# Attention into a maxout layer on one core: other buffers, one group of filler products less and earlier loads of q and k in the first batch

## Chip, core and metric

The kernel runs on one NeuronCore of a Trainium2 chip. The metric is the device time of one execution in microseconds (us), lower is better; the median of the runs counts.

## The reference

Attention with a causal window of 128 positions and a linear position penalty per head, for 8 batches, 8 heads, 576 positions and head size 64, and behind it a maxout layer:

```python
scores = q @ k.T / sqrt(64) - slope[h] * |i - j|      # only 0 <= i - j < 128
attn = softmax(scores)
x = concat_heads(attn @ v)                            # 4608 tokens x 512
h = max(x @ w1, x @ w2, x @ w3)                       # 768 wide
out = h @ w_out                                       # 512 wide
```

All data are float32. The linear layers are done in three products of split operands each (high x low, low x high, high x high).

## The kernel before

A **task** is a pair of heads of one batch (32 tasks, four to a batch, `NP = 4`). A **step** is one block of 128 query rows of a task; the steps of two tasks make 9, so a batch has 18 (`n_steps`). For a step, TensorE makes the score products (`products`, L431; on steps 2, 6, 10 and 14 of a batch whole 128x256 blocks to `ps_m`, else to `ps_s`), VectorE merges the two key blocks by a mask (`score`, L447 and L450) and takes bias and row minimum into a tile `s` (L461), ScalarE makes the exponentials into a tile `p` with their sums (`exps`, L473). For each two steps the sums are inverted (L479, L480) and `p` is scaled, one of the two by GpSimd (L487), the other by ScalarE (L492). Four steps later TensorE transposes `p` (`turn`, L500, into the single PSUM tile `pt`), ScalarE copies it out as `pr` or `pp` (L504, L509, L512), GpSimd cuts it to the window with two selections for a step (L520, L524), and TensorE multiplies with `v` (`mix`, L545, into `ps_x`; L567 in later batches). ScalarE copies the result out as `xk` (L552).

`plain_x` (through `split`, L614 on ScalarE and L615 on VectorE) splits `xk` in a high and a low part `xs`, the right operand of the linear layer. In batches 0 and 1 the layer is done plainly: `plain`, L791, in units of 12 products of 128x288, four units for each of nine groups of weights and eight more for the output layer. The first halves of three units are done early (`begin_early`, L767). From batch 2 on, seven products replace eight (`unit`, L846), with combined weights.

The weights come as 12 groups in int64 words (`fetch`, L152, tile `hs`, two buffers `hs2`) and are turned into floats in pieces between the rest (`preparing`): a clamp (L166 on VectorE, for the later groups L170 and L171 on ScalarE), a conversion (L177, L181), three pieces of bit work (L186), a cast (L200, ScalarE) and a difference (L203, VectorE) into `ring` or `ow`; the floats and the split ones are stored to DRAM (L327, L216).

`spin` (L375) adds products of zeros to `pt`, in fours, whose results nobody reads: at the start, at steps 3, 5, 7 and so on of batch 0, and ten before the second unit of `plain`.

The order of the work is a list of events with due times in steps (`at`, at the end of the function). In batch 0 a scheduler moves instructions from there: it fills each engine's queue by what it believes to be ready, so that buffers and loads change the order. From the due time 46 on (in batch 2) the order on TensorE is that of the list.

q and k of a task lie in one tile `qk` (`load`, L394, two buffers), v in `v` (`load_v`, L399, two buffers). All these loads, the weights' loads and the stores are issued by one queue, SyncE's, in order: a transfer whose buffer is not yet free holds up those behind it. A task's q and k are asked for at step 1 of the task two before, its v at step 3 of the task before. Pools: `s_p` holds `s` (3 buffers), `p` (4) and `pr` (2); `xs_p` has 7 buffers for the factors `xs`; `hq_p` 7 for the hidden units `hq` (128x288); `t_p` 10 for `t` (128x288).

Of the kernel before, what the change touches and what calls it, by code (L numbers as in the profile page):

```python
# [8 lines left out]
F32 = mybir.dt.float32  # L9
# [10 lines left out]
LOAD_I = 1  # L20
# [17 lines left out]
def attention_maxout_kernel(  # L38
# [12 lines left out]
    P = 128  # L51
    B, NP, _, _, S = qk.shape
# [5 lines left out]
    NB = S // P  # L58
# [3 lines left out]
    qk_p = ctx.enter_context(tc.tile_pool(name="qk_p", bufs=2))  # L62
    v_p = ctx.enter_context(tc.tile_pool(name="v_p", bufs=2))
    s_p = ctx.enter_context(tc.tile_pool(name="s_p", bufs=3))
    pp_p = ctx.enter_context(tc.tile_pool(name="pp_p", bufs=4))
    xk_p = ctx.enter_context(tc.tile_pool(name="xk_p", bufs=1))
    xs_p = ctx.enter_context(tc.tile_pool(name="xs_p", bufs=7))
    hq_p = ctx.enter_context(tc.tile_pool(name="hq_p", bufs=7))
    hs_p = ctx.enter_context(tc.tile_pool(name="hs_p", bufs=7))
    t_p = ctx.enter_context(tc.tile_pool(name="t_p", bufs=10))  # L70
# [76 lines left out]
    def raw_tile():  # L147
        return hs_p.tile([P, SMALL + 4 * DM], I32, name="hs2", bufs=2)

    def fetch(g):  # L150
        r = raws[g] = raw_tile()
        nc.sync.dma_start(r[:, SMALL:].bitcast(U8)[:, :16 * DM - 3], w_all[g].bitcast(U8)[:, 3:])  # L152
# [233 lines left out]
    tasks = [(b, hp) for b in range(B) for hp in range(NP)]  # L386
    qkt, vt = {}, {}


    def load(t):  # L390
        b, hp = tasks[t]
        qkt[t] = qk_p.tile([P, 2, S], F32, name="qk")
        for cs in (slice(0, 2 * P), slice(2 * P, S)) if t == 0 else (slice(0, S),):
            nc.sync.dma_start(qkt[t][:, :, cs], qk[b, hp, :, :, cs])  # L394

    def load_v(t):
        b, hp = tasks[t]
        vt[t] = v_p.tile([P, NB + 1, P], F32, name="v")
        nc.sync.dma_start(vt[t], v[b, hp])  # L399

    pn, pp, xp, xk, stats = {}, {}, {}, {}, {}
# [8 lines left out]
    n_steps = len(steps) // B  # L410
# [27 lines left out]
    def score(s):  # L438
        t, i = steps[s]
        b, hp = tasks[t]  # L440
        ps, a = banks.pop(s)
        first = tc.keep_in_program_order if s < 4 else lambda x: x
        if i:
            mask = prev[:, i == NB].bitcast(mybir.dt.uint8)
            if a is None:
                for x in ps:
                    first(nc.vector.copy_predicated(x[:, P:2 * P], mask, x[:, :P]))  # L447
            else:
                both = scores[:, :, a * 2 * P:(a + 1) * 2 * P]
                first(nc.vector.copy_predicated(  # L450
                    both[:, :, P:], mask.unsqueeze(1).broadcast_to([P, 2, P]), both[:, :, :P],
                ))

        if s % 2 == 0:
            stats[s // 2] = st_p.tile([P, 3, 2, 2], F32, name="st")
        st = stats[s // 2]
        less[s] = []
        for j in range(2):
            x = s_p.tile([P, P], F32, name="s", bufs=3)
            below = bias_t[:, hp // 2, j] if i == NB else (bias if i else bias0)[:, 2 * hp + j, :]  # L460
            first(nc.vector.tensor_tensor_reduce(  # L461
                out=x, in0=ps[j][:, P:2 * P], in1=below,
                scale=-0.125, scalar=3.0e38, op0=ALU.add, op1=ALU.min, accum_out=st[:, 0, s % 2, j:j + 1],
            ))
            less[s].append(x)
# [2 lines left out]

    def exps(s):
        st, a = stats[s // 2], s % 2  # L470
        p = pn[s] = s_p.tile([P, 2, P], F32, name="p", bufs=4)
        for j, x in enumerate(less.pop(s)):
            nc.scalar.activation(  # L473
                p[:, j], x, AF.Exp, bias=st[:, 0, a, j:j + 1], scale=-1.0, accum_out=st[:, 1, a, j:j + 1]
            )
# [134 lines left out]
    xs, hs, hq = {}, {}, {}  # L610
# [261 lines left out]
    def at(when, what, *args):  # L872
        events.append((when, len(events), what, args))
# [2 lines left out]
    where = {x: s for s, x in enumerate(steps)}  # L876
    for s, (t, i) in enumerate(steps):
        c = s + shift[tasks[t][0]]
        if i == LOAD_I and t + 2 < len(tasks):
            at(c - 0.4, load, t + 2)  # L880
        if i == NB - 1 and t + 1 < len(tasks):
            at(c - 0.4, load_v, t + 1)
        if i == 0 and 0 < t < NP:
            at(c - 1, slopes, t)
            if t % 2 == 0:
                at(c - 1, slopes_t, t // 2)
        at(c + 0.04, score, s)
        at(c + 0.3, exps, s)
        if s % 2 == 0:
            at(c + 0.002, products, s)  # L890
            at(c + DRAIN[0].get(n_steps - s, LAG_T) + 0.003, turn, s)
        else:
            at(c + (0.6 if s == n_steps - 1 else 1.1), sums_of, s)
            at(c + (0.8 if s == n_steps - 1 else 1.5), normalise, s)
# [34 lines left out]
    at(2.06, weights, 1)  # L929
    for s in range(5, n_steps + 2):  # L930
        at(s + 0.2, weights, 1.4 if s > 5 else 0.6)
    for s in range(3, n_steps, 2):
        at(s + 0.45, spin, SPIN)

    def fix():
# [3 lines left out]
    at(2 * n_steps + LAG_X + shift[2], fix)  # L939
    spin(FIRST_SPIN)  # L940
    load(0)
    nc.scalar.dma_start(dist[:, 2], c_ident)
    fetch(0)
    slopes(0)
    slopes_t(0)
    load(1)
    load_v(0)
    nc.scalar.copy(out=plus, in_=dist[:, 2])
    fetch(1)
    for _, _, what, args in sorted(events, key=lambda e: e[:2]):  # L950
        what(*args)

# [37 lines left out]
```

## Time and profile before

| | |
|---|---|
| median of 3 runs | 750.1 us (749.47 to 752.38) |
| the profiled execution | 752.57 us, span from first to last instruction 750.9 us |
| mean granted TensorE clock | 0.995 of full speed |
| TensorE products, busy | 733.9 us (98%) |
| TensorE weight loads, busy | 674.6 us (90%) |
| VectorE, ScalarE, GpSimd, busy | 515.2, 487.2 and 236.4 us |
| DMA | 192.81 MB, mean 257 GB/s |

The span has three parts: the attention of batch 0 until about 57 us, the plain layer of batches 0 and 1 mixed with the attention of later batches, and the layer with combined weights. PE is TensorE's products, PEld its weight loads, DVE VectorE, ACT ScalarE, POOL GpSimd, SPq the queue of SyncE. TensorE's busy time is modelled from starts, since products overlap. float32 products of `L431`, `L500` and `L545` appear as two records each in the trace.

### The profile page before, as it was taken

How to read it: one execution, taken by the hardware profiler on the slowest of the kernel's cores; microseconds unless marked ns; L12 is line 12 of the kernel's file. 1: busy time of each engine (PE TensorE's matmuls, PEld its weight loads, DVE VectorE, ACT ScalarE, POOL GpSimd, SP SyncE). 2: the span in 40 equal slices, each digit the busy share in tenths (PEclk: the TensorE clock that was granted, in tenths of full speed). 3: DMA queues.
4: the chain of work that ended last, by engine and by line, in shares of the span. 5: the costliest groups of instructions: out<-in, count | busy, mean ns of one | idle time of the engine just before them, and what ended most of it. 6: DMA issues, size and time to landing. Idle time of an engine off the chain costs nothing.

```text
span 750.9 us, 19281 instructions
## 1 busy us (share of the span) xinstructions
PE 733.9 (98%) x7209; PEld 674.6 (90%) x7214; DVE 515.2 (69%) x1614; ACT 487.2 (65%) x1603; POOL 236.4 (31%) x451
## 2 busy tenths in 40 slices
PE   7999989999999999999999999999999999999998
PEld 3459988999999999999999999999999999999998
DVE  4888887536659477784778567794777747683673
ACT  5786976766667767676677757776666767552342
POOL 4661224645556123212222123222222122343100
PEclk8999999999999999999999999999999999999999
DMA  7877999759998489855988378864988468899611
GB/s 252 274 282 298 330 340 331 253 187 340 361 349 275 134 279 303 273 181 192 322 294 276 116 266 304 291 213 146 330 289 273 163 228 272 252 291 355 230 61 64
DMA packets 57085, 192.81 MB, mean 257 GB/s; under 512 B 5792, under 2 KB 24480, under 8 KB 50464
## 3 DMA queue, kind: packets, MB, share of 16 engines
q0 software_dynamic: 20304, 108.54, 43.9%
q1 hardware_dynamic: 36400, 82.85, 31.2%
q8 instruction: 57, 0.93, 0.5%
q14 instruction: 36, 0.29, 0.1%
q10 hardware_dynamic: 288, 0.20, 0.1%
HBM read 156.95 MB, written 34.60 MB: 255 GB/s over the span
## 4 chain that ended last, share of the span: by engine, by line
PE 77%; DVE 11%; ACT 7%; DMA 2%; issue 1%; POOL 1%; SPq 0%; DVEq 0%; ACTq 0%; POOLq 0%
PE ps_m L846 46%; PE ps_m L791 16%; PE ps_s L431 5%; PE pt L500 4%; PE ps_x L567 4%; DVE hs L615 2%; DVE hq L733 2%; ACT p L473 2%; DVE t L732 2%; DMA qk<-in_qk 1%; PE ps_x L545 1%; DMA hs<-in_w_all 1%; ACT p L492 1%; DVE t L618 1%; DVE xs L615 1%
## 5 line engine op out<-in xcount | busy, mean ns | idle before, releaser
L846 PE MATMUL ps_m<-xs,ring 128*128 128x288 f32 x2160 | 302.7, 297 | 0.6
L846 PEld LDWEIGHTS ps_m<-xs,ring 128*128 128x128 f32 x2160 | 290.1, 188 | 3.7 <-ACT t L863 3.4
L520 POOL TENSOR_SCALAR_AFFINE_SELECT pp<-pr 128x256 f32<-128x256 f32 x112 | 53.9, 482 | 277.2 <-ACT pr L504 154.0
L473 ACT ACTIVATE p<-s,st 128x128 f32<-128x128 f32 x288 | 114.7, 400 | 20.8 <-DVE st L461 17.2
L863 ACT COPY t<-ps_m 128x288 f32<-128x288 f32 x196 | 76.7, 394 | 71.2 <-PE ps_m L846 69.5
L791 PE MATMUL ps_m<-xs,ring 128*128 128x288 f32 x846 | 118.1, 297 | 2.8 <-DVE hq L808 2.2
L791 PEld LDWEIGHTS ps_m<-xs,ring 128*128 128x128 f32 x846 | 113.3, 188 | 4.1 <-DVE hq L808 2.4
L367 POOL DMA_DIRECT2D ring<-keep x103 | 55.5, 539 | 165.5 <-PE ps_m L846 157.3
L846 PE MATMUL ps_m<-hs,ow 128*128 128x288 f32 x756 | 105.8, 297 | 0.4
L846 PEld LDWEIGHTS ps_m<-hs,ow 128*128 128x128 f32 x756 | 100.9, 188 | 2.6 <-ACT t L863 1.2
L492 ACT ACTIVATE p<-p,st 128x128 f32<-128x128 f32 x252 | 84.6, 393 | 24.1 <-DVE st L480 24.1
L732 DVE TENSOR_TENSOR t<-ps_m,t 128x288 f32<-128x288 f32 x108 | 48.8, 453 | 42.8 <-PE ps_m L846 32.5
L461 DVE CUSTOM_DVE_ANT_0 s<-ps_s,bias 128x128 f32<-128x128 f32 x240 | 60.6, 285 | 9.0 <-POOL bias_t L112 3.4
L431 PE MATMUL ps_s<-qk 64*64 64x192 f32 (+1 forms) x1088 | 62.0, 319 | 3.4 <-DMA qk<-in_qk 2.4
L614 ACT CAST hs<-hq 128x288 fp32r<-128x288 f32 x96 | 40.2, 432 | 30.8 <-DVE hq L733 18.1
L473 ACT ACTIVATION_READ_ACCUMULATOR p<-s,st 128x1 f32 x288 | 55.3, 192 | 0.0
L567 PE MATMUL ps_x<-pp,v 64*64 64x64 f32 (+3 forms) x1456 | 53.4, 274 | 0.1
L567 PEld LDWEIGHTS ps_x<-pp,v 64*64 64x64 f32 x1456 | 41.7, 133 | 10.5 <-issue 8.6
L500 PE MATMUL pt<-plus,p 128*128 128x128 f32 x288 | 48.5, 289 | 2.0 <-POOL p L487 1.3
L524 POOL TENSOR_SCALAR_AFFINE_SELECT pp<-pr 128x256 f32<-128x256 f32 (+1 forms) x112 | 50.0, 447 | 1.1
L733 DVE TENSOR_TENSOR hq<-t,hq 128x288 f32<-128x288 f32 x108 | 48.8, 457 | 2.1
L601 DVE TENSOR_TENSOR xk<-ps_x,xk 128x256 f32<-128x256 f32 (+3 forms) x56 | 25.4, 454 | 36.0 <-ACT xk L600 36.0
(94 smaller groups left out, 942.0 us busy)
## 6 DMA issues: line engine op xcount, KB each, us to landing
ring<-keep POOLq DMA_DIRECT2D x51, 1024.0 KB, 7.4
ring<-keep POOLq DMA_DIRECT2D x61, 768.0 KB, 6.1
qk<-in_qk SPq DMA_DIRECT2D x31, 576.0 KB, 5.3
hs<-in_w_all SPq DMA_DIRECT2D x12, 1023.6 KB, 7.2
v<-in_v SPq DMA_DIRECT2D x32, 320.0 KB, 6.5
outT<-t SPq DMA_DIRECT2D x64, 144.0 KB, 1.8
keep<-ring SPq DMA_DIRECT2D x9, 768.0 KB, 6.5
plain<-hs SPq DMA_DIRECT2D x12, 512.0 KB, 4.0
```

The lines of the kernel that those rows point to most:

```text
L367: nc.gpsimd.dma_start(wts[n, a], keep[n % 9][a])
L431: pe(nc.tensor.matmul(ps[j][d:d + D, o:o + k1 - k0], lhsT=qkt[u][j * D:(j + 1) * D, 0, q0:q0 + D], rhs=qkt[u][j * D:(j + 1) * D, 1, k0:k1] ...
L461: first(nc.vector.tensor_tensor_reduce(out=x, in0=ps[j][:, P:2 * P], in1=below, scale=-0.125, scalar=3.0e38, op0=ALU.add, op1=ALU.min, acc ...
L473: nc.scalar.activation(p[:, j], x, AF.Exp, bias=st[:, 0, a, j:j + 1], scale=-1.0, accum_out=st[:, 1, a, j:j + 1])
L492: nc.scalar.activation(p[:, j], p[:, j], AF.Copy, scale=st[:, 2, a, j:j + 1])
L500: pe(nc.tensor.transpose(out=pt[:, a, j], in_=p[:, j], identity=ident))
L567: pe(nc.tensor.matmul(x[j * D:(j + 1) * D, r, o:o + rhs.shape[1]], lhsT=vv[k, i, j * D:(j + 1) * D], rhs=rhs[k], start=start, stop=True, s ...
L732: nc.vector.tensor_tensor(out=s, in0=ps, in1=e, op=ALU.add)
L733: nc.vector.tensor_tensor(out=h, in0=s, in1=h, op=ALU.max)
L791: pe(nc.tensor.matmul(ps, lhsT=lt, rhs=rt, start=n == 0 and not (b == 0 and v < EARLY), stop=n == len(pairs) - 1, skip_group_check=True,))
L846: pe(nc.tensor.matmul(part_of[n, {2: 0, 5: 0, 6: 0, 3: 1}.get(kk, kk)], lhsT=lt, rhs=rt, start=first, stop=i == len(pairs) - 1, skip_group ...
L863: nc.scalar.copy(out=e, in_=ps)
```

## The change

In batch 0 the tile `s` is taken from `hq_p` (7 buffers) and `p` from `t_p` (10 buffers), which nothing else uses there yet. The filler products of step 5 go. q and k of tasks 2 and 3 are loaded at the beginning, to two of the factors' seven buffers, and with them v of task 1; the loads of the steps keep tasks 4 and up. In the changed file the lines from `load` on are one higher, from `exps` on two higher (L394 is L395, L431 is L432, L473 is L475, L487 is L489, L500 is L502, L545 is L547, L615 is L617, L767 is L769, L791 is L793).

```diff
     def load(t):
         b, hp = tasks[t]
-        qkt[t] = qk_p.tile([P, 2, S], F32, name="qk")
+        own = 2 <= t < NP
+        qkt[t] = (xs_p if own else qk_p).tile([P, 2, S], F32, name="xs" if own else "qk")
...
         for j in range(2):
-            x = s_p.tile([P, P], F32, name="s", bufs=3)
+            x = s_p.tile([P, P], F32, name="s", bufs=3) if b else hq_p.tile([P, P], F32, name="hq")
...
         st, a = stats[s // 2], s % 2
-        p = pn[s] = s_p.tile([P, 2, P], F32, name="p", bufs=4)
+        first = s < n_steps
+        p = pn[s] = t_p.tile([P, 2, P], F32, name="t") if first else s_p.tile([P, 2, P], F32, name="p", bufs=4)
...
-        if i == LOAD_I and t + 2 < len(tasks):
+        if i == LOAD_I and NP <= t + 2 < len(tasks):
             at(c - 0.4, load, t + 2)
-        if i == NB - 1 and t + 1 < len(tasks):
+        if i == NB - 1 and 1 < t + 1 < len(tasks):
             at(c - 0.4, load_v, t + 1)
...
-    for s in range(3, n_steps, 2):
+    for s in [3, *range(7, n_steps, 2)]:
         at(s + 0.45, spin, SPIN)
...
     load(1)
     load_v(0)
     nc.scalar.copy(out=plus, in_=dist[:, 2])
+    load(2)
+    load_v(1)
     fetch(1)
+    load(3)
```

The order changes on every engine in batch 0. Three places matter below.

TensorE around step 5, before: the last score products of step 5 (`ps_m_301`) stand behind the four filler products, and the transposes of steps 2 and 3 alternate with the products with v.

```order
L431 MATMUL ps_m_301<-qk 64x256 x2
L500 MATMUL pt<-plus,p 128x128 x2
L545 MATMUL ps_x<-pp,v 64x256
L500 MATMUL pt<-plus,p 128x128 x2
L545 MATMUL ps_x<-pp,v 64x256
L431 MATMUL ps_s<-qk 64x192 x4
L431 MATMUL ps_s<-qk 64x128 x3
```

The same place after the change:

```order
L432 MATMUL ps_m_295<-qk 64x256 x2
L432 MATMUL ps_m_296<-qk 64x256 x2
L547 MATMUL ps_x<-pp,v 64x256 x2
L502 MATMUL pt<-plus,t 128x128 x2
L432 MATMUL ps_s<-qk 64x192
L502 MATMUL pt<-plus,t 128x128
L432 MATMUL ps_s<-qk 64x192 x2
L502 MATMUL pt<-plus,t 128x128
```

No filler stands there now, and the products with v stand ahead of the transposes.

TensorE near the end of batch 0's attention, before: two of the four transposes of steps 14 and 15 stand behind the 18 early products (L767).

```order
L431 MATMUL ps_s<-qk 64x192 x7
L500 MATMUL pt<-plus,p 128x128 x2
L767 MATMUL ps_m_651<-xs,ring 128x288 x6
L767 MATMUL ps_m_658<-xs,ring 128x288 x6
L767 MATMUL ps_m_665<-xs,ring 128x288 x6
L500 MATMUL pt<-plus,p 128x128 x2
```

After:

```order
L432 MATMUL ps_s<-xs 64x192 x5
L502 MATMUL pt<-plus,t 128x128 x4
L769 MATMUL ps_m_660<-xs,ring 128x288 x2
L769 MATMUL ps_m_646<-xs,ring 128x288 x6
L769 MATMUL ps_m_653<-xs,ring 128x288 x6
L769 MATMUL ps_m_660<-xs,ring 128x288 x4
```

All four transposes stand ahead of the early products now.

VectorE at the last two steps of batch 0 (16 and 17), before: the reciprocal of their sums (L480, the second one here) stands ahead of the bit work on the weights.

```order
L461 ISA s,st<-ps_s,bias 128x128
L461 ISA st 128x1
L166 TENSOR_SCALAR hs_482<-hs_482 128x1024
L177 ISA hs_482<-hs_482 128x1024
L480 RECIPROCAL st<-st 128x4
L186 SCALAR_TENSOR_TENSOR hs_482<-hs_482 128x256
L186 SCALAR_TENSOR_TENSOR hs_482<-hs_482 128x512
L186 SCALAR_TENSOR_TENSOR hs_482<-hs_482 128x256
L203 TENSOR_TENSOR ow<-hs_482,ow 128x2x256 x2
```

After:

```order
L177 ISA hs_477<-hs_477 128x1024
L462 ISA hq,st<-ps_s,bias 128x128
L462 ISA st 128x1
L186 SCALAR_TENSOR_TENSOR hs_477<-hs_477 128x256
L462 ISA hq,st<-ps_s,bias 128x128
L462 ISA st 128x1
L186 SCALAR_TENSOR_TENSOR hs_477<-hs_477 128x512
L186 SCALAR_TENSOR_TENSOR hs_477<-hs_477 128x256
L203 TENSOR_TENSOR ow<-hs_477,ow 128x2x256 x2
L482 RECIPROCAL st<-st 128x4
```

The same weights' work (L177, L186, L203) now lies among the last scores and ahead of the reciprocal.

## Rows read from the trace of the kernel before

**Rows 1.** Windows: length; busy PE, PEld, DVE, ACT, POOL; granted clock, DMA share, GB/s.
```profile
0.00:57.00 57.00, 48.83 (x361) 24.17 (x366) 41.08 (x148) 41.04 (x150) 32.80 (x58) 0.94 0.77 269
57.00:136.00 79.00, 74.58 (x798) 69.12 (x802) 63.42 (x189) 59.19 (x174) 22.66 (x43) 1.00 0.91 328
136.00:750.00 614.00, 610.44 (x6058) 581.29 (x6048) 410.73 (x1279) 387.01 (x1279) 180.97 (x351) 1.00 0.74 247
```
**Rows 2.** Timeline of PE, 55 to 140 us: start, us, instructions [idle before].
```profile
57.52 4.27 PE L791 MATMUL ps_m<-xs,ring 128*128 128x288 f32 x30 [0.63 <-DVE xs L615]
...
104.14 1.86 PE L791 MATMUL ps_m<-xs,ring 128*128 128x288 f32 x12 [2.17 <-DVE hq L808]
```
**Rows 3.** Timeline of PE around steps 3 to 9.
```profile
11.26 1.34 PE L431 MATMUL ps_s<-qk 64*64 64x192 f32 x14 [2.41 <-DMA qk<-in_qk]
12.53 1.11 PE L500 MATMUL pt<-plus,p 128*128 128x128 f32 x4
13.57 1.97 PE L431 MATMUL ps_m<-qk 64*64 64x256 f32 x12
15.48 0.61 PE L375 MATMUL pt<-hs 128*128 128x512 bf16 x1
16.30 1.06 PE L375 MATMUL pt<-hs 128*128 128x512 bf16 x2 [0.22 <-issue]
...
18.86 0.44 PE L500 MATMUL pt<-plus,p 128*128 128x128 f32 x2
...
28.33 0.66 PE L500 MATMUL pt<-plus,p 128*128 128x128 f32 x4
```
**Rows 4.** Windows of 1 us around the fall and return of the clock.
```profile
10.00:11.00 1.00, 0.00 (x0) 0.00 (x0) 1.00 (x5) 0.26 (x1) 0.29 (x2) 0.79 1.06 441
11.00:12.00 1.00, 0.74 (x11) 0.59 (x14) 0.52 (x5) 1.00 (x5) 0.40 (x1) 0.50 1.04 439
...
17.00:18.00 1.00, 1.00 (x6) 0.32 (x6) 0.00 (x0) 0.00 (x0) 0.00 (x0) 0.79 0.00 0
```
**Rows 5.** Timeline of POOL: a normalisation in batch 0, and the last steps.
```profile
22.10 2.06 POOL L487 TENSOR_TENSOR p<-p,st 128x256 f32<-128x256 f32 x2
...
46.42 1.17 POOL L520 TENSOR_SCALAR_AFFINE_SELECT pp<-pr 128x256 f32<-128x256 f32 x1 [1.12 <-ACT pr L504]
...
49.60 0.61 POOL L487 TENSOR_TENSOR p<-p,st 128x256 f32<-128x256 f32 x1
```
**Rows 6.** Timeline of PE at the early products.
```profile
42.85 2.66 PE L767 MATMUL ps_m<-xs,ring 128*128 128x288 f32 x18 [0.18 <-DVE xs L615]
45.34 0.38 PE L500 MATMUL pt<-plus,p 128*128 128x128 f32 x2
```
**Rows 7.** Timeline of DVE: second weights' clamp, and from step 15 to the split.
```profile
22.92 0.77 DVE L166 TENSOR_SCALAR hs<-hs 128x1024 int8<-128x1024 int8 x1
...
38.56 0.29 DVE L461 CUSTOM_DVE_ANT_0 s<-ps_m,bias 128x128 f32<-128x128 f32 x1 [0.43 <-ACT p L473]
...
39.55 1.65 DVE L203 TENSOR_TENSOR ow<-hs,ow 128x512 fp32r<-128x512 f32 x2 [0.69 <-ACT ow L200]
...
47.39 0.18 DVE L480 RECIPROCAL st<-st 128x4 f32<-128x4 f32 x1
47.49 1.75 DVE L186 SCALAR_TENSOR_TENSOR hs<-hs 128x256 uint32<-128x256 uint32 x3
50.10 1.50 DVE L203 TENSOR_TENSOR ow<-hs,ow 128x512 fp32r<-128x512 f32 x2 [0.86 <-ACT ow L200]
...
55.19 1.20 DVE L177 CUSTOM_DVE_ANT_0 hs<-hs 128x1024 int32<-128x1024 int8 x1
```
**Rows 8.** Timeline of ACT: the casts of the weights behind the split.
```profile
59.11 1.15 ACT L200 CAST ow<-hs 128x512 fp32r<-128x512 f32 x2
```
**Rows 9.** The chain that ended last, two pieces on PE: start, us.
```profile
61.78 0.48 PE ps_s L431 x6
...
68.85 0.44 PE pt L500 x4
```

## Prediction
> **What bounds the kernel now.** I read the windows of the span first, then TensorE's timeline, then the timelines of the engines for which it waits. The windows [rows 1] split the span in three. From 136 us on PE works 610.44 of 614 us: whatever the change does there, only the moment counts at which this stretch begins, and the order of its instructions hardly changes. Between 57 and 136 us PE works 74.58 of 79 us, so 4.42 us are idle, 2.17 of them in one wait at 104.14 [rows 2]. Before 57 us it works 48.83 of 57, and the clock is 0.94. So the layer's units, which begin at 57.52 [rows 2], are bound by PE, and the attention of batch 0 by a chain of short steps through all engines. A gain must come from an earlier 57.52, from work that is already done by then, or from the 4.42 us.
>
> **The added products of step 5.** PE has made 12 of the 16 score products of step 5 by 15.54; then the four added products hold it to 17.36, and only then come the last four score products [rows 3]. All this is at the lower level of the clock, 1.2 GHz (granted 0.50); it fell in the window from 10 to 11 us, when PE waited for q and k, and returned in that from 17 to 18, both of which show 0.79 [rows 4]: at about 10.6 and 17.4. Without the added products the 16 score products end at 13.57 + 16 x 0.164 = 16.2 (1.97 us for 12 [rows 3]). Next stand four records of products with v, in front of the transposes and no longer between them. No row shows them at the low clock; I price them as score products of the same 256 columns, 4 x 0.164 = 0.66, which gives 16.86. Then the four transposes, 1.11 us at the low clock and 0.66 at the full one, with eight records of score products between them, 0.096 each at the low clock (1.34 us for 14 [rows 3]) and about half at the full one. They end at 18.0 if the clock is full at once and at 18.7 if it stays low; with the return at 17.4, as before, at 18.2. Before they ended at 18.86 + 0.44 = 19.3 [rows 3]. So they are **1.1 us earlier**, between 0.6 and 1.3. Behind them follow a copy on ACT, four selections and two normalisations on POOL, at 22.10 for 2.06 us [rows 5], and transposes that wait for these; the order there is unchanged, so I let the 1.1 us pass on to the end of batch 0.
>
> At one place a rule speaks against this. The granted clock came back only after a stretch in which the added products stood [rows 4]. The Trainium skill (TensorE: Matmul & The Clock Gate, Part 4: PE-mode transpose) says that transposes do not count as activity for the clock gate as other products do. By it the transposes that now come at 16.9 would help less than the products removed, and the return would be later; by the sum above that alone costs 0.5 us (18.7 for 18.2). What a much later return would do is a rival below.
>
> **The end of batch 0.** Before, the 18 early products held PE from 42.85, and two transposes of steps 14 and 15 stood behind them, at 45.34 [rows 6]; so POOL's selections of these steps began at 46.42, and the normalisation of steps 16 and 17, ready from the reciprocal at 47.39 on [rows 5, 7], began only at 49.60 [rows 5], behind them. Now all four transposes stand ahead of the early products, so POOL is done with those selections some 2.7 us (one length of the 18 [rows 6]) sooner, beside the 1.1. What is late next is the reciprocal itself: VectorE's order now puts the three pieces of bit work, 1.75 us, and the two differences, 1.50 us [rows 7], ahead of it. At best, if VectorE is that far ahead by then, it comes at 47.39 - 1.1 = 46.3; at worst at 46.3 + 3.25 = 49.5. VectorE had waits of 0.43 us (for ScalarE to free an `s`) and 0.69 us (for a cast) shortly before [rows 7], which the work moved forward can fill; I take 49.5 - 1.1 = 48.4, near the worst, since these are the only gaps I can point to. That is 1.2 us before the 49.60 at which the normalisation began. The rest of the way to the first unit (transposes, selections, products with v, copy, split) I leave as long as it was: the conversion of 1.20 us that stood on VectorE before the split [rows 7] is done earlier, but two casts of 1.15 us [rows 8], which stood behind the split, are now ahead of it on ScalarE. So the units begin at 57.52 - 1.2 = 56.3, between 54.2 (3.3 earlier) and 57.4 (0.1 earlier).
>
> **Work that is done by then.** Six records of score products and four transposes of batch 1 stood behind the first units, 0.48 and 0.44 us [rows 9]; the order now has them ahead of the first unit, in time that PE spends on fillers and on its wait of 0.63 us [rows 2]. That is 0.9 us less behind it; at worst PE reaches its first unit later by as much, and it is nothing.
>
> **The loads.** After 11.26 no product waits for q or k [rows 3], so the earlier loads alone gain nothing directly. They put 0.9 MB ahead of the second weights: at 439 GB/s [rows 4] those land 2 us later, and their first user stands at 22.92 [rows 7], behind work that ends long after. Cover: VectorE's order; if it were gone, 2 us. In return the later queue has two loads less between the weights, and the weights' work runs ahead. I book nothing for it.
>
> **The buffers.** What the trace shows of waits for `s` is the 0.43 us above; for `p` none is named. Where the order stays, more buffers change nothing; what they do, they do through the order. The later splits of batch 1 take two buffers that tasks 2 and 3 have long left: nothing.
>
> **The sum.** 1.2 + 0.9 = 2.1 us. The profiled execution took 752.57 us (span 750.9), 2.5 above the median; on its own terms it becomes 750.5, and the median 750.1 - 2.1 = **748.0 us**. With the bounds (0.1 + 0 to 3.3 + 0.9) it lies between 745.9 and 750.0. A measurement of this kernel tells about 0.5% from no change, 3.75 us: below 746.35 is faster, above 753.85 slower.
>
> **Rivals.**
> - The weights' work ahead also takes the waits out of the stretch from 57 to 136 us. For it: VectorE's share there is 63.42 of 79 us [rows 1], the wait of 2.17 us is for VectorE [rows 2], and it has some 3 us of weights' work less then (1.75 + 1.50). Against it: the units take these weights in turn, and two buffers for raw weights still tie each load to a store. With two thirds of the 4.42 us the time is 748.0 - 3.0 = 745.0.
> - The new order gives all of it back: reciprocal at its worst, split later by the casts, units at 57.4 with nothing ahead, or waits behind them that grow by as much as was won. For it: scores and reciprocal of the last steps now queue behind weights' work that has no haste. It gives 750, between 749.3 and 751. This is also the case in which buffers and loads do not do what they say.
> - Slower: the clock does not return at 17.4. Full-speed transposes take 0.66 us where low ones take 1.11 [rows 3], so of each us at the low clock 0.4 is lost where PE is the bound. To end at 753.85 the 2.1 us and 3.75 more must go: 5.9 / 0.4 = 14.6 us, so the clock would have to stay low until 32 us. The fillers of steps 7, 9 and 11 remain and speak against it: the return at 17.4 came right behind fillers. With a return at 36 us it would be 748.0 + 18.6 x 0.4 = 755.4.
>
> **How the numbers follow.** Forecast 0.48, waits gone too 0.24, all given back 0.20, clock 0.05, something else 0.03. Faster by over 0.5%: most of the second case and the edge of the first, 0.27. Slower: 0.06. Within: 0.67. The range takes in the bounds of the forecast and the third case, and the second down to a little below its 745.0: 744.6 to 751.0; it leaves out the clock case, the lowest part of the second and the unnamed, under 0.2.
>
> **What would show it.** Right: no products of L375 between 13.6 and 19 us; transposes of steps 2 and 3 done by about 18.2 and a clock of 1.00 from 18 on; four transposes ahead of the early products, reciprocal of the last steps near 48.4, first unit near 56.3, and from 136 us on the same length as before. Wrong: a clock of 0.50 beyond 18 us; a first unit at 57.5 or later; the idle time from the first unit to 136 us far from 4 us, either way; a last stretch of another length.

## The result and the profile after

The change makes the kernel **slower**: 756.15 us (755.15 to 757.51, 4 runs) against 750.91 us (749.47 to 752.38, 4 runs), ratio 1.0068 with a 95% interval of 1.0043 to 1.0093. A second measurement of the same kernel, with 12 runs (e10 below), gave 1.0056 (1.0033 to 1.0078). The prediction was 748.0 us in a range of 744.6 to 751.0.

The windows of the span after answer to [rows 1]. Columns: window, length, busy time of TensorE, its weight loads, VectorE, ScalarE and GpSimd with their instructions, granted clock, DMA share, GB/s.

```profile
0.00:57.00 57.00, 43.28 (x326) 22.09 (x330) 39.51 (x147) 38.44 (x145) 30.66 (x55) 0.94 0.75 273
57.00:136.00 79.00, 73.96 (x762) 66.58 (x763) 62.47 (x183) 57.89 (x166) 23.79 (x40) 1.00 0.85 308
136.00:750.00 614.00, 612.84 (x6103) 583.72 (x6102) 412.58 (x1287) 390.16 (x1293) 183.34 (x357) 1.00 0.74 248
```

TensorE does 5.55 us less before 57 us (43.28 for 48.83), and little of it is won back later. Its timeline says where, beginning with the answer to [rows 2] (start, length, engine, line, operation, count, idle time before and what ended it):

```profile
12.62 0.77 PE L432 MATMUL ps_s<-qk 64*64 64x192 f32 x14 [4.23 <-DMA qk<-in_qk]
14.36 1.99 PE L432 MATMUL ps_m<-qk 64*64 64x256 f32 x16
16.28 0.83 PE L547 MATMUL ps_x<-pp,v 128*64 128x256 f32 x4
18.61 0.33 PE L502 MATMUL pt<-plus,t 128*128 128x128 f32 x1
23.64 1.26 PE L502 MATMUL pt<-plus,t 128*128 128x128 f32 x4 [2.42 <-POOL t L489]
62.79 10.66 PE L793 MATMUL ps_m<-xs,ring 128*128 128x288 f32 x78
109.81 1.85 PE L793 MATMUL ps_m<-xs,ring 128*128 128x288 f32 x12 [2.29 <-DVE hq L810]
141.41 8.86 PE L793 MATMUL ps_m<-hs,ow 128*128 128x288 f32 x65
```

The first unit stands at 62.79, 5.27 us later than before [rows 2], and the first unit of the output layer at 141.41, where before it was 136.60: of the 5.27 us 0.46 come back. The wait of [rows 2] at 104.14 is still there, at 109.81. From the output layer to the end nothing changes (755.8 - 141.41 = 614.4, before 750.9 - 136.60 = 614.3).

VectorE's timeline at the end of batch 0, first before (the reciprocals of steps 12 and 13 and of 14 and 15; that of 16 and 17 is the 47.39 of [rows 7]), then after:

```profile
41.32 0.16 DVE L480 RECIPROCAL st<-st 128x4 f32<-128x4 f32 x1
44.37 0.17 DVE L480 RECIPROCAL st<-st 128x4 f32<-128x4 f32 x1
```

```profile
43.00 0.17 DVE L482 RECIPROCAL st<-st 128x4 f32<-128x4 f32 x1
43.27 1.83 DVE L617 TENSOR_TENSOR xs<-xk,xs 128x576 fp32r<-128x576 f32 x2
...
46.43 0.83 DVE L166 TENSOR_SCALAR hs<-hs 128x1024 int8<-128x1024 int8 x1
47.18 0.16 DVE L482 RECIPROCAL st<-st 128x4 f32<-128x4 f32 x1
...
47.58 1.21 DVE L177 CUSTOM_DVE_ANT_0 hs<-hs 128x1024 int32<-128x1024 int8 x1
...
48.92 0.42 DVE L186 SCALAR_TENSOR_TENSOR hs<-hs 128x256 uint32<-128x256 uint32 x1
...
49.47 1.35 DVE L186 SCALAR_TENSOR_TENSOR hs<-hs 128x512 uint32<-128x512 uint32 x2
51.97 1.43 DVE L203 TENSOR_TENSOR ow<-hs,ow 128x512 fp32r<-128x512 f32 x2 [1.15 <-ACT ow L200]
53.32 0.16 DVE L482 RECIPROCAL st<-st 128x4 f32<-128x4 f32 x1
```

From the reciprocal of steps 12 and 13 to that of 16 and 17 it was 6.07 us and is 10.32. In between now stand the whole bit work of a conversion (L186), a wait of 1.15 us for a cast on ScalarE, and the two differences (L203).

GpSimd behind that reciprocal, first before (its normalisation at 49.60 is in [rows 5]; two selections like these stand between the two), then after:

```profile
51.84 0.40 POOL L520 TENSOR_SCALAR_AFFINE_SELECT pp<-pr 128x256 f32<-128x256 f32 x1
...
52.92 0.41 POOL L524 TENSOR_SCALAR_AFFINE_SELECT pp<-pr 128x256 f32<-128x256 f32 x1
```

```profile
53.57 0.61 POOL L489 TENSOR_TENSOR t<-t,st 128x256 f32<-128x256 f32 x1 [1.32 <-DVE st L482]
...
55.93 1.39 POOL L526 TENSOR_SCALAR_AFFINE_SELECT pp<-pr 128x256 f32<-128x256 f32 x1
57.28 0.58 POOL L522 TENSOR_SCALAR_AFFINE_SELECT pp<-pr 128x256 f32<-128x256 f32 x1
57.81 0.85 POOL L526 TENSOR_SCALAR_AFFINE_SELECT pp<-pr 128x256 f32<-128x256 f32 x1
```

From the normalisation to the first unit it was 7.92 us and is 9.22. The last four selections of batch 0 took 1.63 us and take 3.23 (the first of the four, at 55.57, took 0.41). e10 has the same four lengths; in e12 below, with another order, each takes 0.41 again.

Last, SP's queue: when the loads of q and k are issued. Before, the two of tasks 4 and 5, the first of batch 1, go out at 32.65 and 42.21; after, they follow the early ones at 13.20 and 19.43 (one row of 6.56 us, with the wait in between), since tasks 0 and 1 leave both buffers and tasks 2 and 3 no longer take them. The prediction had not looked at these two loads.

```profile
32.65 0.33 SPq L394 DMA_DIRECT2D qk<-in_qk  x1
42.21 0.33 SPq L394 DMA_DIRECT2D qk<-in_qk  x1
```

```profile
13.20 6.56 SPq L395 DMA_DIRECT2D qk<-in_qk  x2
```

### The profile page after: what moved, and what is told of

The parts are those of the page before. It is cut to its first block, busy times and chain, and to the rows that moved or that the text cites. A ratio compares the mean times of both kernels' runs of the same rounds, so it can differ in the third digit from the quotient of the medians.

```text
span 755.8 us, 19256 instructions
## 1 busy us (share of the span) xinstructions
PE 732.6 (97%) x7206; PEld 674.6 (89%) x7210; DVE 515.5 (68%) x1614; ACT 486.9 (64%) x1603; POOL 237.8 (31%) x451
## 4 chain that ended last, share of the span: by engine, by line
PE 72%; DVE 11%; ACT 5%; DMA 3%; issue 1%; POOL 0%; SPq 0%; ACTq 0%; DVEq 0%; POOLq 0%
PE ps_m L848 45%; PE ps_m L793 14%; PE ps_s L432 4%; PE ps_x L569 4%; PE pt L502 4%; DMA hs<-in_w_all 2%; DVE hs L617 2%; DVE hq L735 2%; DVE t L734 2%; ACT p L475 1%; DVE t L620 1%; ACT p L494 1%; DMA plain<-hs 1%; DVE hs L186 1%; DVE hs L181 1%
## 5 line engine op out<-in xcount | busy, mean ns | idle before, releaser
L793 PE MATMUL ps_m<-xs,ring 128*128 128x288 f32 x846 | 117.4, 297 | 2.3 <-DVE hq L810 2.3
L793 PEld LDWEIGHTS ps_m<-xs,ring 128*128 128x128 f32 x846 | 113.2, 188 | 3.3 <-DVE hq L810 2.5
L475 ACT ACTIVATE p<-s,st 128x128 f32<-128x128 f32 x252 | 100.5, 401 | 17.6 <-DVE st L462 15.4
L494 ACT ACTIVATE p<-p,st 128x128 f32<-128x128 f32 x234 | 78.7, 394 | 23.5 <-DVE st L482 23.5
L432 PE MATMUL ps_s<-qk 64*64 64x192 f32 (+1 forms) x1048 | 58.0, 316 | 5.6 <-DMA qk<-in_qk 4.2
L462 DVE CUSTOM_DVE_ANT_0 s<-ps_s,bias 128x128 f32<-128x128 f32 x224 | 56.6, 286 | 6.3 <-ACT p L475 3.7
L526 POOL TENSOR_SCALAR_AFFINE_SELECT pp<-pr 128x256 f32<-128x256 f32 (+1 forms) x112 | 52.8, 472 | 1.1
L451 DVE COPY_PREDICATED ps_s<-prev,ps_s 128x256 f32<-128x256 uint8 x105 | 44.4, 423 | 7.4 <-PE ps_s L432 5.8
L475 ACT ACTIVATION_READ_ACCUMULATOR p<-s,st 128x1 f32 x252 | 48.5, 192 | 0.0
```

The lines of the kernel that those rows point to most:

```text
L432: pe(nc.tensor.matmul(ps[j][d:d + D, o:o + k1 - k0], lhsT=qkt[u][j * D:(j + 1) * D, 0, q0:q0 + D], rhs=qkt[u][j * D:(j + 1) * D, 1, k0:k1] ...
L462: first(nc.vector.tensor_tensor_reduce(out=x, in0=ps[j][:, P:2 * P], in1=below, scale=-0.125, scalar=3.0e38, op0=ALU.add, op1=ALU.min, acc ...
L475: nc.scalar.activation(p[:, j], x, AF.Exp, bias=st[:, 0, a, j:j + 1], scale=-1.0, accum_out=st[:, 1, a, j:j + 1])
L494: nc.scalar.activation(p[:, j], p[:, j], AF.Copy, scale=st[:, 2, a, j:j + 1])
L793: pe(nc.tensor.matmul(ps, lhsT=lt, rhs=rt, start=n == 0 and not (b == 0 and v < EARLY), stop=n == len(pairs) - 1, skip_group_check=True,))
```

## How the runs are compared

Two sorts of scatter lie over differences of a few us. The first is when q and k of task 1 land: TensorE's products for them began at 11.26 us in the profile before, at 12.62 after, and between 10.50 and 12.54 in the others that load them behind the first weights. The second is the clock: each timed run lists its mean granted clock, and one straight line through all 289 timed runs (a level for each kernel, one slope for all) gives 5.6 us for 0.01 of it, with 1.0 us left around it. So each experiment has its ratio, and in the table its **level at clock 1.00**, a worked-out number with a 95% interval of about 0.65 us (0.3 for before, 1.1 for the first four runs after, 1.0 for e11 and e13). It rests on that line, not on a control of the clock, and what a version should cost through its clock is left out of it and stands in the ratio alone. The experiments e1 to e15 are described below the table.

| kernel | ratio to before (95%) | median us | mean clock | level at 1.00 | 12/13 to first unit | 12/13 to output layer |
|---|---|---|---|---|---|---|
| before | 1 | 752.1 | 0.9956 | 749.4 | 16.20 | 95.28 |
| e10, the change | 1.0056 (1.0033-1.0078) | 756.31 | 0.9938 | 752.7 | 20.90 | 98.11 |
| e1 buffers alone | 1.0001 (0.9986-1.0017) | 752.62 | 0.9960 | 750.3 | 16.26 | 95.55 |
| e2 no fillers at 5 alone | 1.0007 (0.9988-1.0026) | 752.56 | 0.9947 | 749.8 | 15.35 | 95.49 |
| e3 early loads alone | 1.0034 (1.0014-1.0053) | 755.34 | 0.9955 | 752.6 | 20.75 | 98.45 |
| e4 all but the fillers | 1.0049 (1.0027-1.007) | 754.84 | 0.9945 | 752.1 | 21.32 | 98.49 |
| e5 change, batch 1's loads held | 1.001 (0.999-1.003) | 752.74 | 0.9942 | 749.6 | 15.35 | 96.20 |
| e6 as e5, fillers kept | 1.0023 (1.0006-1.0039) | 753.8 | 0.9929 | 750.1 | 15.35 | 95.94 |
| e7 weights' work written later | 1.0066 (1.0043-1.0089) | 757.86 | 0.9950 | 754.4 | 17.98 | 99.22 |
| e8 the same, pinned | 1.0033 (1.0012-1.0054) | 754.3 | 0.9950 | 751.6 | 16.56 | 95.66 |
| e11 two steps more of it | 1.0085 (1.0057-1.0114) | 757.84 | 0.9937 | 754.4 | 17.77 | 102.70 |
| e12 early loads, order of e5 | 1.0024 (1.0006-1.0041) | 753.76 | 0.9937 | 750.1 | 15.37 | 95.95 |
| e13 held loads, order of the change | 1.0134 (1.0099-1.0168) | 760.51 | 0.9893 | 755.2 | 21.19 | 102.38 |
| e14 VectorE's order of e5 | 1.0018 (0.9995-1.0041) | 752.27 | 0.9972 | 751.4 | 15.67 | 97.07 |
| e9 q and k of task 1 first | 0.9986 (0.9966-1.0005) | 750.53 | 0.9969 | 749.1 | 16.20 | 95.14 |
| e15 the same again | 0.9996 (0.9976-1.0017) | 751.64 | 0.9956 | 749.2 | 16.20 | 94.63 |

The last two columns are times between rows of one profile: from the reciprocal of steps 12 and 13 on VectorE to TensorE's first unit, and to the first unit of the output layer. They leave out the start, where q and k and the clock scatter, and with it what an order costs ahead of that reciprocal: e8 has 95.66, nearly as before, and a level 2.1 us higher. In the first profile after they are 19.79 and 98.41.

## The experiments: which part it is

**e1** takes the two lines on `s` and `p` alone, **e2** the line on the fillers, **e3** all lines on the loads; **e4** is the whole change but the line on the fillers.

> The kernel before with the extra buffers for s and p alone. My theory: the loss needs the early loads into the factors' buffers, so this one is equal to the kernel before within 0.3% (750.9, from 749.0 to 752.5), its first unit stands near 57.5 us and the reciprocal of the last steps near 47.4; the order of the engines does not move. The rival, that the buffers themselves let weights' work go ahead of the last scores: 753 or more, first unit at 59 or later.

> The kernel before without the added products of step 5 alone. My theory: q and k of task 1 still come at 11.3, the transposes of steps 2 and 3 end about 0.4 to 1.1 us earlier (18.2 to 18.9), and of that little reaches the end: 750.9, from 749.5 to 751.5, the clock 1.00 from 18 to 30 us. The rival, that the removed products are what lets the clock fall a second time at 23 us: granted clock of 0.50 in some window between 22 and 27, first unit at 58.5 or later, 752 to 753.

> The kernel before with the early loads of q, k and v of batch 0 alone, two of them to the factors' buffers; fillers and buffers for s and p as before. My theory: this part holds nearly all of the loss. q and k of task 1 land 1.4 us later (first product of its scores at 12.6 for 11.3), and the weights' conversion stands ahead of the last scores and of the last reciprocal (53 for 47.4): first unit at 61 to 63 us, 754.5 to 756.5. The rival, that the loss needs the fillers removed or the buffers too: 751 to 753.5.

> The whole change, but with the added products of step 5 kept. My theory: they hold the clock only a little; 754.5 to 756.5, first unit at 61 to 63. The rival, that their removal costs 1.2 us or more by the second fall of the clock at 23 us: here no window between 22 and 27 us is below 0.90, and the time is 1.2 us or more under that of the whole change, 755.0 or less, with the first unit at 61.6 or earlier.

Buffers alone and fillers alone change nothing that can be measured. The early loads alone cost 0.34%, and their profile has the picture of the whole change, a last reciprocal at 50.62 and a first unit at 61.14:

```profile
11.02 1.23 PE L432 MATMUL ps_s<-qk 64*64 64x192 f32 x14 [1.72 <-DMA qk<-in_qk]
61.14 9.03 PE L792 MATMUL ps_m<-xs,ring 128*128 128x288 f32 x66
```

```profile
40.39 0.16 DVE L481 RECIPROCAL st<-st 128x4 f32<-128x4 f32 x1
...
49.26 1.44 DVE L203 TENSOR_TENSOR ow<-hs,ow 128x512 fp32r<-128x512 f32 x2 [1.10 <-ACT ow L200]
50.62 0.17 DVE L481 RECIPROCAL st<-st 128x4 f32<-128x4 f32 x1
```

One half of my theory fell here. I had read the 1.36 us by which q and k of task 1 came later after the change as the early loads taking their bandwidth. But e3 has these loads and gets q and k at 11.02; e1 has none of them and gets them late:

```profile
12.54 0.77 PE L431 MATMUL ps_s<-qk 64*64 64x192 f32 x14 [3.79 <-DMA qk<-in_qk]
```

It is scatter between executions, not the change.

The fillers. In e2 the clock falls a second time, as after the change: granted 0.66 and 0.50 from 23 to 25 us, behind a time in which TensorE waits for GpSimd's normalisation.

```profile
23.00:24.00 1.00, 0.45 (x2) 0.29 (x2) 0.45 (x5) 0.00 (x0) 0.50 (x1) 0.66 1.00 395
24.00:25.00 1.00, 1.00 (x6) 0.53 (x6) 0.22 (x2) 0.73 (x4) 0.22 (x1) 0.50 1.05 432
```

```profile
22.53 0.44 PE L500 MATMUL pt<-plus,p 128*128 128x128 f32 x2 [1.61 <-POOL p L487]
23.55 0.69 PE L500 MATMUL pt<-plus,p 128*128 128x128 f32 x2 [0.58 <-POOL p L487]
```

In the profiles of before, e1, e3, e4 and e6, with the fillers, it does not fall there. Yet e2 is no slower: its first unit is at 57.20. So the rival in e2's expectation was right that the clock falls, but no price shows at the end. Nor do the fillers alone decide: e15 below keeps them and falls at 22 us, e7 leaves them out and has full clock from 16 to 40 us. e3 came out 0.15% under e4, inside the intervals.

## The experiments: how the loads do it

**e5** is the change with the loads of tasks 4 and 5 held at their written place in SP's queue; **e6** keeps the fillers as well.

```
-            nc.sync.dma_start(qkt[t][:, :, cs], qk[b, hp, :, :, cs])
+            x = nc.sync.dma_start(qkt[t][:, :, cs], qk[b, hp, :, :, cs])
+            if NP <= t < NP + 2:
+                tc.keep_in_program_order(x)
```

> The whole change, but the loads of q and k of tasks 4 and 5, which belong to batch 1, are held at their old place in SP's queue instead of going out at 13 us into the buffers that are now free. My theory: it is these two loads that make batch 1's work ready early and so put the weights' conversion ahead of batch 0's last scores; without them the last reciprocal comes 6.0 to 6.6 us after that of steps 12 and 13 (6.07 before, 10.32 in the whole change), the first unit 16 to 17 us after it (16.2 before, 19.8 in the whole change), and the time is within 0.3% of the kernel before. The rival, that the loss comes from the transfers of q, k and v at the start or from the buffers: 0.4% or more slower than before, as the whole change is.

> As the one before, and the added products of step 5 kept. My theory: no second fall of the clock at 23 us, the end of batch 0 as in the kernel before; within 0.3% of it. The rival, that the fillers' removal is worth its 1.1 us at the end once the order is right: 0.15% slower than the one before. A second rival, that the second fall of the clock is paid at the end: 0.15% or more faster than the one before.

This undoes the loss: 1.001, and 749.6 us at clock 1.00 for 752.7. All of the change is in it, the early loads of batch 0 too; only the time of the two loads is different, and the order that the scheduler made. The two loads go out at 32.61 and 50.80; from reciprocal to reciprocal it is 3.12 and 3.08 us, as before (3.05 and 3.02), and to the first unit 15.35:

```profile
32.61 0.44 SPq L395 DMA_DIRECT2D qk<-in_qk  x1
...
50.80 0.42 SPq L395 DMA_DIRECT2D qk<-in_qk  x1
```

```profile
42.18 0.16 DVE L484 RECIPROCAL st<-st 128x4 f32<-128x4 f32 x1
45.30 0.17 DVE L484 RECIPROCAL st<-st 128x4 f32<-128x4 f32 x1
48.38 0.18 DVE L484 RECIPROCAL st<-st 128x4 f32<-128x4 f32 x1 [0.25 <-ACT st L483]
```

Neither of e6's rivals is shown: 749.6 and 750.1 at equal clock, each within 0.7.

**e7** writes the weights' work of steps 14 to 17 behind batch 0's last normalisation; **e8** does so and pins each of these instructions behind what is written ahead of it; **e11** starts at step 12.

```
-        at(s + 0.2, weights, 1.4 if s > 5 else 0.6)
+        at(s + 0.2 if s < 14 else n_steps + 0.01 * s, weights, 1.4 if s > 5 else 0.6)
```

> The whole change, with the weights' work of steps 14 to 17 written behind the last normalisation of batch 0; the two differences with their wait for a cast (1.15 + 1.43 us) then stand behind the last reciprocal, the conversion before them still ahead. My theory, that VectorE's order in front of that reciprocal is the loss: it comes 7.5 to 8.2 us after that of steps 12 and 13 (10.32 in the whole change), the first unit about 2 to 2.6 us earlier, and the time is 0.2% to 0.35% under that of the whole change, so 0.35% to 0.5% over the kernel before. The rival, that the weights' work is needed by the first units and only moves its wait: as slow as the whole change, 0.6% to 0.9% over.

> As the one before, and this weights' work also pinned behind what is written ahead of it, so that on VectorE all of it stands behind the last reciprocal of batch 0. My theory: the reciprocal comes 6 us or less after that of steps 12 and 13, the first unit 3.5 to 4.3 us earlier than in the whole change, and the time is that of the kernel before within 0.3%. The rival, that the weights come late for the units of the first layer: a new wait of 2 us or more between 57 and 136 us and a time 0.5% or more over the kernel before.

> As e8, with the weights' work of steps 12 and 13 held back too, so that the conversion with the cast wait of 1.95 us, which in the whole change and in e8 stands in front of the reciprocal of steps 12 and 13, stands behind the last reciprocal as well. My theory, that e8 is still slower than the kernel before at equal clock because of this one: the reciprocal of steps 12 and 13 comes 1 to 1.5 us earlier than in e8 (40.96), the time is 0.15% under that of e8. The rival, that two conversions behind the last reciprocal are too much: the first layer's units wait for weights or for VectorE between 57 and 136 us, and the time is 0.2% or more over that of e8.

The reciprocals of e7 and e8 moved much as expected, but the time did not follow. In e7 the last reciprocal comes 8.38 us after that of steps 12 and 13 (10.32 in the change) and the first unit 1.8 us sooner than in the first profile of the change, but the units up to the output layer take 81.24 us for 78.62: no gain, its rival held, and at equal clock it is 1.7 us over the change. In e8 the last reciprocal is 6.13 us behind, the first unit 16.56, and the level is 1.1 us under the change, still 2.1 over before; 1.0033 lies between what its theory (within 0.3%) and its rival (0.5% or more) asked for. e11 loses more: the reciprocal of steps 12 and 13 comes at 41.77, not earlier than in e8 (40.96, but there q and k came 1.48 us sooner; counted from them it is 0.67 us earlier), and its units wait for VectorE and for weights.

```profile
74.00 0.77 PE L439 MATMUL ps_s<-qk 64*64 64x192 f32 x16 [2.09 <-DVE st L469]
76.13 0.69 PE L800 MATMUL ps_m<-xs,ring 128*128 128x288 f32 x2 [0.94 <-ACT ring L206]
```

So "the weights' conversion stands in front of the last reciprocal" is what the trace shows, but pushing that work back is no cure: it must be done before 136 us too.

What was left was order or transfers: with the two loads the order of all engines moves, and e5 changes both at once. **e12** and **e13** cross them. A loop at the end of the kernel goes through a list of each engine's instructions and ties each to the one before it in the list; the tie sets the order and waits for nothing. So it holds TensorE, VectorE, ScalarE and GpSimd to the order of another kernel (e5 for e12, the whole change for e13) up to the first units of the output layer. In **e14** the list holds VectorE alone.

```
+    def in_order():
...
+                    if last is not None:
+                        tc.add_manual_dep(i, last, info, reason="order")
+                    last = i.name
```

> The whole change, its loads with it (tasks 4 and 5 at 13 us too), but TensorE, VectorE, ScalarE and GpSimd are held to the order that they have in e5, up to the first units of the output layer. My theory, that the loss is the order alone and not the transfers: reciprocal of steps 12 and 13 at 41 to 42.5, from it to the first unit 15.4 us and to the output layer 95.5 to 96.5 as in e5, within 0.3% of the kernel before. The rival, that q and k of tasks 4 and 5 at 13 us disturb other transfers: 0.35% or more over the kernel before with the same order.

> The reverse: the loads of tasks 4 and 5 held back as in e5, but the four engines held to the order that they have in the whole change. My theory: the loss is there in full, 98.4 us from the reciprocal of steps 12 and 13 to the output layer, 0.35% to 0.8% over the kernel before. The rival: the time of e5, within 0.25% of the kernel before.

> The whole change, with VectorE alone held to its order of e5; the other engines are free, and ScalarE's order stays different from both. My theory, that VectorE's order is what matters: within 0.3% of the kernel before, 95.5 to 96.5 us from the reciprocal of steps 12 and 13 to the output layer. The rival, that ScalarE's casts ahead of the copies and exponentials carry the loss (VectorE waited 1.95 us for one): 0.35% or more over the kernel before.

e12 has both loads from 13.42 on and the order of e5, and runs as e5 does: 15.37 us to the first unit, 95.95 to the output layer, 750.1 at clock 1.00 (e5 749.6, the change 752.7).

```profile
13.42 7.45 SPq L452 DMA_DIRECT2D qk<-in_qk  x2
```

```profile
43.82 0.16 DVE L539 RECIPROCAL st<-st 128x4 f32<-128x4 f32 x1
46.94 0.17 DVE L539 RECIPROCAL st<-st 128x4 f32<-128x4 f32 x1
50.02 0.18 DVE L539 RECIPROCAL st<-st 128x4 f32<-128x4 f32 x1 [0.25 <-ACT st L538]
```

```profile
59.19 4.26 PE L850 MATMUL ps_m<-xs,ring 128*128 128x288 f32 x30
```

Its plain ratio of 1.0024 lies between e5's 1.001 and the change's 1.0056. Its mean clock is that of e10 (0.9937 and 0.9938), so that the 2.55 us between their medians need no line. e13 has the late loads and the change's order, and the loss is there, and more: 21.19 us to the first unit, as in e10 and e3, then a new wait. The chain in front of that wait leads back to a load of weights that went out at 73.21, right behind a load of q and k; its like in the change went out at 70.42. SyncE's queue was not held to any list, so this further loss, and with it part of e13's level, belongs to the crossing and not to the change.

```profile
90.13 1.34 PE L491 MATMUL ps_s<-qk 64*64 64x192 f32 x16 [4.44 <-DVE st L521]
```

That settles it: **with the same loads, the order makes 2.6 of the 3.3 us (e10 against e12, 1.7 to 3.4); the early transfers cost nothing that can be told (e12 against e5, 0.5 us, -0.3 to 1.3)**. Between e12 and the kernel before 0.7 us (0.1 to 1.3) are left without a cause. VectorE's order alone (e14) gives back 1.3 us (0.5 to 2.2), with the other engines free; its 97.07 us to the output layer miss its theory's 96.5. Which share ScalarE's and TensorE's orders hold was not tried.

## The experiments: the fillers in the change, and the start

> The whole change again, for more runs with their clocks: with e4 it tells what the fillers of step 5 are worth inside the change. My theory: 0.45% to 0.7% over the kernel before; at equal mean clock the same as e3 and e4 within 0.1%, since the removal gains as much in front of the transposes as the second fall of the clock costs. The rival, that the removal costs 1.2 us by that fall: 0.15% or more over e4.

e10 is the change as it is. At equal clock it is 752.7, e4 752.1 and e3 752.6, each within 0.65: the fillers' removal is neither a gain nor a loss inside the change that these runs can tell. Its mean clock is 0.9938 for 0.9956 before, which by the line is 1.0 us; with the 3.3 us of the levels that is about the 4.2 us of the medians. The plain ratios, with the clock in them, say the same of the fillers: e10 and e4 lie 0.07% apart, e5 and e6 0.13% the other way.

**e9** and **e15** try the wait for q and k that all profiles have, in the kernel before:

```
-    at(2.06, weights, 1)
+    at(2.2, weights, 1)
...
+    load(1)
     fetch(0)
     slopes(0)
     slopes_t(0)
-    load(1)
```

> The kernel before, with q and k of task 1 loaded ahead of the first weights and the first piece of weights' work written behind the first reciprocal. My theory of the start: TensorE waits there for q and k of task 1, at 11.0 to 12.6 us in all runs so far, with or without the early loads, because the first weights share the DMA engines with them; ahead of the weights they land by 10, the wait of 1.6 to 4.3 us shrinks to under 1, the clock doesn't fall at 11 to 13, the reciprocal of steps 12 and 13 comes at 38.5 to 40 (41.3 to 41.9 in the kernel before and in two runs that keep its loads), and the time is 0.15% to 0.5% under the kernel before. The rival, that the weights' work then comes late on VectorE and takes it back: within 0.1%.

> e9 once more, since its gain of 0.14% was not resolved: q and k of task 1 ahead of the first weights in the kernel before. My theory: 0.1% to 0.3% under the kernel before, with a mean clock above that of the kernel before. The rival: no difference, within 0.1% either way.

The wait is gone, the products go on at 8.51, and in e9's profile the clock is 1.00 all the way to 57 us, the first unit at 54.38 and the span 747.8:

```profile
8.51 0.77 PE L431 MATMUL ps_s<-qk 64*64 64x192 f32 x16
10.71 0.66 PE L500 MATMUL pt<-plus,p 128*128 128x128 f32 x4 [1.43 <-POOL p L487]
...
54.38 4.27 PE L791 MATMUL ps_m<-xs,ring 128*128 128x288 f32 x30 [0.63 <-DVE xs L615]
```

But over 24 runs the ratios are 0.9986 and 0.9996, both with 1 inside their intervals; e15's profile has the clock low from 12 to 16 and again from 22 to 26 us. No version tried is shown to beat the kernel before.

## Why the prediction was wrong

- **The loads, "I book nothing for it".** That the transfers themselves cost nothing held as far as it can be told (e12). What the prediction did not ask is whose buffers they free: tasks 2 and 3 in the factors' buffers leave the two for q and k to batch 1, whose loads then go out at 13.20 and 19.43 instead of 32.65 and 42.21. With the loads some 20 us sooner the scheduler makes another order, in which the weights' work stands ahead of batch 0's last reciprocal. Batch 1's scores do not stand there: ahead of 53.32 VectorE's rows write `hq`, batch 0's tile, and `s` only from 53.41 on. By which of its rules the scheduler does so is not shown. The prediction read the new order on TensorE and VectorE, but took it for a gain; the next two points show where that failed.
- **The reciprocal of the last steps, "48.4", at worst 49.5: the step that failed.** Measured 53.32, 4.92 us later than forecast and 5.93 later than before, so that the 1.2 us booked as won were a loss. The bounds had the bit work and the differences (3.25 us) ahead of it, and rightly so. But they were counted from a start 1.1 us early, and the reciprocal of steps 12 and 13 came 1.68 us late (q and k came 1.36 late, so that most of this can be their scatter); between it and that of 14 and 15 a clamp of weights (0.83) and a longer split (1.83 for 1.46) make it 1.13 us more (4.18 for 3.05); and behind that stand bit work, differences and their wait of 1.15 us for a cast, so that it is 6.14 for 3.02. 47.39 + 1.68 + 1.13 + 3.12 = 53.32. The wait was in the rows before, with 0.86 us [rows 7], and the 3.25 left it out. "Near the worst" was chosen for want of gaps to fill; what VectorE would newly wait for was not asked.
- **The first unit, "56.3": 62.79.** The way to it was left at 7.92 us from the normalisation on (57.52 - 49.60). It took 9.22, 1.3 us more; the four last selections on GpSimd alone took 1.6 us more. Why they did is open: VectorE has a clamp and a conversion of weights beside them (54.85 to 57.06), but nothing here tests that. Over the way from the reciprocal of steps 12 and 13, which leaves most of that scatter out, the change loses 4.70 us in e10 (20.90 for 16.20).
- **The fillers of step 5, "1.1 us earlier", passed on.** Half right. No added products stand there (the four records with v took 0.83 us for the 0.66 priced), the clock was back at about 16.7 without them, and the four transposes of steps 2 and 3 ended at 18.94 for 19.3, though q and k came 1.36 us later. But nothing was passed on: GpSimd's normalisation, behind its selections, began at 22.42 for 22.10 [rows 5], TensorE stood idle for 2.42 us before 23.64, and the clock fell again (0.50 from 24 to 26 us). e2 has the same without the loads, and no gain. The Trainium skill (TensorE: Matmul & The Clock Gate, Part 4: PE-mode transpose) says that transposes do not count for the clock as other products do, and by it the return should have been later without the fillers; the trace does not show that (0.66 granted from 16 to 17 us, where before 0.79 stood at 17 to 18 [rows 4]), but the fall was later too, so it is no test.
- **Work ahead, 0.9 us.** The order held: 78 products of units follow the first one without a break. From the first unit to the output layer it is 0.46 us less after, 1.4 in e3, 1.9 in e4 and in e10, so the term had about the right size. With it, e10's loss of 4.70 us is 2.8 at the output layer, beside the 3.3 by the levels.
- **The buffers: nothing.** Right: e1 is at 1.0001.
- **The rivals.** The "slower" rival had about the right size (753.85 to 755.4) by luck: its cause, the clock not returning at 17.4, did not come about. "The new order gives all of it back" had the right kind of cause, the order (VectorE's holds 1.3 us of it), and stopped at zero: it allowed the order to eat the gain, but not to cost more than the gain. That the waits from 57 to 136 us would go did not happen: TensorE's idle time from the first unit to the output layer is 3.94 us, before 3.90.

## What to carry to other kernels

A load moved to a spare buffer also frees the buffer it used to take: follow that one to its next user, and ask what a scheduler will do with loads that go out 20 us sooner. Order is a cost of its own; to price it, cross it with the thing that moved it (same loads, other order), since pushing back the instruction that seems in the way may only move the wait. Where executions differ by 0.5% through the clock, compare times between rows inside one profile, and levels at equal clock, before a single span.

## What the runs showed that I had not expected

- The granted clock goes with most of the scatter: of the 33 runs of the kernel before that stood beside e5 to e8, the five with a mean of 1.000 took 748.3 to 749.4 us but for one of 752.7, the four at 0.990 or 0.991 took 753.6 to 755.6.
- A wait alone does not tell whether the clock falls. Before, it fell behind a wait of 2.41 us [rows 3]; in e14 a longer one (2.64 us, to 10.96) was followed by full clock up to 22 us, in e5 a shorter one (1.75 us, to 11.05) by 0.50 from 12 on.
- A fall at 104 to 110 us, behind the wait of about 2.2 us there, costs nothing that can be seen at the output layer: from the end of that wait to the output layer it is 32.39 us in e1 with such a fall (0.50 from 106 to 108) and 32.46 before without.
